# Reordered head loads and units, a later z row and fold, a fold over four PSUM banks, and a split last block in a four-layer transformer kernel

## Chip, cores and metric

The kernel runs on one core of one Trainium2 chip. The metric is the device time of one execution in microseconds (us). Executions of one kernel here differ by up to 0.2%, so each comparison below rests on several executions of both kernels on the same chip. All executions told of are fast: none is over 1.5% above the fastest of its kernel. Each execution also has a span, from its first to its last instruction, which lies 1.9 to 2.6 us under its time, and a clock, the mean share of its full speed that TensorE was granted.

## The reference, cut to what matters

`x` is 2048 tokens by 1024 channels in bf16. Two linear-attention blocks alternate with two gated feed-forward blocks, each behind a layernorm and with a residual.

```python
def _A_ref(x, wqkv, wo):                      # 32 heads of 32
    q, k, v = split_heads(x @ wqkv)
    phi = lambda t: jnp.where(t > 0, t + 1, jnp.exp(t)) + 1e-6
    pq, pk = phi(q), phi(k)
    kv = jnp.einsum("bhsd,bhse->bhde", pk, v)
    z = jnp.einsum("bhsd->bhd", pk)
    num = jnp.einsum("bhqd,bhde->bhqe", pq, kv)
    den = jnp.einsum("bhqd,bhd->bhq", pq, z)[..., None] + 1e-6
    return merge_heads(num / den) @ wo
def _B_ref(x, W_gate, W_up, W_down):
    return (relu(x @ W_gate) * (x @ W_up)) @ W_down
x = x + _A_ref(_layernorm(x), A_wqkv, A_wo);  x = x + _B_ref(_layernorm(x), ...)   # twice
```

## The kernel before

TensorE does all products; a unit is a 128 x 512 output, eight matmuls of 512 columns. `x` is cut into 16 blocks of 128 tokens. In the first layer the head loads weights and `x` in an order chosen by hand, normalizes the first four blocks on VectorE, transposes them on TensorE and starts the value units:

```python
        k0, k1, v0, v1 = (ring.place() for _ in range(4))
        self.load_x(0, 0)
        self.load_x(0, 1)
        v0(0, H)
        self.load_x(1)
        v0(H, 2 * H)
        v1()
        self.load_x(2)
        self.load_x(3)
        k0()
        self.load_x(4)
        # ... (cut) x 5 to 7, k1, x 8 to 15
        with tc.manual_schedule(engines={mybir.EngineType.DVE, mybir.EngineType.Activation}):
            for j in range(QT):                    # the first four blocks
                for c in range(2):
                    self.ln_stat(j, src[j], c, stats[j])
                r = self.ln_rstd(stats[j])
                # ... (cut) scale and transpose
```

A key unit is evicted in three steps, `exp` on ScalarE, then two on VectorE; the last one writes `pkv`, which the matmuls of `kv_step` read. GpSimd adds the keys up in `ksum`. A query unit takes three ScalarE steps and one on VectorE:

```python
            nc.scalar.activation(out=e, in_=ps, func=ACT.Relu, scale=-1.0)
            nc.scalar.activation(out=e, in_=e, func=ACT.Exp, scale=-1.0)
            nc.scalar.activation(out=e, in_=e, func=ACT.Identity, bias=self.eps6[:, 0:1])
            nc.vector.scalar_tensor_tensor(out=pq[:, c * NW:(c + 1) * NW], in0=ps, scalar=0.0,
                                           in1=e, op0=ALU.max, op1=ALU.add)
```

`z_row` casts `ksum` on ScalarE (`hi`) and spreads it with two matmuls of ones. `fold_wo` multiplies the transposed kv into the output weights: sixteen matmuls, two after each of eight query units, whose results are copied out of PSUM alternately by VectorE and ScalarE. `later.at(n, f)` runs `f` after n further units.

```python
        def fold_wo(i):
            n2, g = divmod(i, G)
            # ... (cut)
            ps = self.ps3.tile([P, NW], F32, tag="b")          # two banks
            nc.tensor.matmul(ps, lhsT=kvT[:, g, :], rhs=ring.get((l, f"o{n2}"))[:, g, :],
                             start=True, stop=True)
            dst = T[g // 2][:, g % 2, n2 * NW:(n2 + 1) * NW]
            if g % 2:
                nc.scalar.activation(out=dst, in_=ps, func=ACT.Copy)
            else:
                nc.vector.tensor_copy(out=dst, in_=ps)
        # ... (cut)
        with self.tc.manual_schedule(engines={mybir.EngineType.DVE,mybir.EngineType.Pool}):
            ring.free_before((l, "v0"))
            later.at(4, z_row)
            run(q_of(0, 4), v_then_kv(2))
            # ... (cut)
            def with_fold(u, i):
                return lambda: (u(), fold_wo(2 * i), fold_wo(2 * i + 1))

            run(q2[:5])
            run([with_fold(u, i) for i, u in enumerate(q2[5:] + q3[:5])])
            run(q3[5:], out0[:3])
            run(out0[3:])
```

Where `manual_schedule` names an engine, the instructions inside it keep the order of the program in that engine's queue (others can still be put between them); elsewhere the framework's scheduler orders it by a model of its own. Either way each engine's order is fixed before the kernel runs.

Of the kernel before, what the change touches and what calls it, by code (L numbers as in the profile page):

```python
# [7 lines left out]
ALU = mybir.AluOpType  # L8
ACT = mybir.ActivationFunctionType
F32 = mybir.dt.float32  # L10
BF16 = mybir.dt.bfloat16
PSUM = bass.MemoryType.PSUM
P = 128
# [65 lines left out]
class _Net:  # L79
# [85 lines left out]
    def head(self):  # L165

        nc, tc, ring = self.nc, self.tc, self.ring
        H = self.KT // 2

        zero = self.ep.tile([P, NW], BF16, tag="e")  # L170
        nc.vector.memset(zero, 0.0)
        idle = self.ps3.tile([P, NW], F32, tag="b")
        for _ in range(10):
            nc.tensor.matmul(idle, lhsT=zero[:, 0:P], rhs=zero, start=True, stop=True)
# [4 lines that stand above are left out]
        v0(0, H)  # L179
        self.load_x(1)  # L180
        v0(H, 2 * H)
        v1()
        self.load_x(2)
        self.load_x(3)
        k0()
        self.load_x(4)
        self.load_x(5)
        self.load_x(6)
        self.load_x(7)
        k1()  # L190
        for t in range(8, self.ST):
            self.load_x(t)
        ring.load_to(5)
        src = self.xb
        self.xnT[0, 0] = self.xnTp.tile([P, self.KT, QT * P], BF16, tag="xnT", name="xnT0_0")
        stats = [self.small.tile([P, 2, nc.vector.BN_STATS_DIM], F32, tag="stats", name=f"st{j}")
                 for j in range(QT)]

        def turn(j, xn, h):
            tp = self.ps3.tile([P, H, P], BF16, tag="b")  # L200
            for i in range(H):
                kt = h * H + i
                nc.tensor.transpose(tp[:, i, :], xn[:, kt * P:(kt + 1) * P], self.ident)
            dst = self.xnT[0, 0][:, h * H:(h + 1) * H, j * P:(j + 1) * P]
            if h == 0:
                nc.vector.tensor_copy(out=dst, in_=tp)
            else:
                nc.scalar.activation(out=dst, in_=tp, func=ACT.Copy)

        with tc.manual_schedule(engines={mybir.EngineType.DVE, mybir.EngineType.Activation}):  # L210
            for j in range(QT):
                for c in range(2):
                    self.ln_stat(j, src[j], c, stats[j])
                r = self.ln_rstd(stats[j])
                xn = self.xnp.tile([P, self.D], BF16, tag="xn")
                for h in range(2):
                    if j == 0 or h == 0:
                        self.ln_scale(src[j], *r, xn, h if j == 0 else None)
                    turn(j, xn, h)

    def ln_turn(self, layer, t, xn):
# [42 lines left out]
    def layer_A(self, l, last_ln):  # L264
# [107 lines left out]
        def fold_wo(i):  # L372
            n2, g = divmod(i, G)
            if n2 == 0 and g % 2 == 0:
                T.append(self.slab.tile([P, 2, D], BF16, tag="slab", name=f"T{l}_{g // 2}"))
            ps = self.ps3.tile([P, NW], F32, tag="b")
            nc.tensor.matmul(ps, lhsT=kvT[:, g, :], rhs=ring.get((l, f"o{n2}"))[:, g, :],
                             start=True, stop=True)
            dst = T[g // 2][:, g % 2, n2 * NW:(n2 + 1) * NW]
# [4 lines that stand above are left out]
# [19 lines left out]
        def q_of(sc, lag):  # L403
            return [lambda j=j, c=c: q_unit(sc, j, c, lag) for j in range(QT) for c in range(H)]
# [4 lines left out]
        def v_then_kv(q):  # L409
            u = column_major(v_unit, q)  # L410

            def last(j):
                u_j = u[QT + j]
                return lambda: (u_j(), later.at(2, lambda: kv_step(q * QT + j)))

            return u[:QT] + [last(j) for j in range(QT)]
# [10 lines left out]
        def run(*lists):  # L427

            n = max(len(u) for u in lists)
            for i in range(n):  # L430
                for u in lists:
                    if i < len(u):
                        u[i]()
                        later.tick()
# [7 lines left out]
        first = column_major(v_unit, 0)  # L442
        if l == 0:

            first = [first[c * QT + j + i] for i in (0, 2) for c in range(H) for j in range(2)]
        run(first)
        run(k_then_kv(0))
        run(column_major(v_unit, 1))
# [5 lines left out]
        run(k3[QT:])  # L454
        with self.tc.manual_schedule(engines={mybir.EngineType.DVE,mybir.EngineType.Pool}):
            ring.free_before((l, "v0"))
            later.at(4, z_row)
            run(q_of(0, 4), v_then_kv(2))
            run(q_of(1, 1), v_then_kv(3))
            ring.free_slowly((l, "q0"), later, 4)  # L460
            later.at(2, finish_kv)
            q2, q3, out0 = q_of(2, 1), q_of(3, 1), out_of(0)

            def with_fold(u, i):
                return lambda: (u(), fold_wo(2 * i), fold_wo(2 * i + 1))

            run(q2[:5])
            run([with_fold(u, i) for i, u in enumerate(q2[5:] + q3[:5])])
            run(q3[5:], out0[:3])
            run(out0[3:])  # L470
            ring.free_slowly((l, "o0"), later, 4)
            self.ln_later(last_ln, 0, 5, 4, 3)
            for sc in range(1, self.NQ):
                run(out_of(sc))
# [12 lines left out]
    def layer_B(self, l, final):  # L487
        nc, KT, D = self.nc, self.KT, self.D
        ring, later = self.ring, self.later
        for q in range(self.NQ):  # L490
            if q + 1 < self.NQ:
                self.ln_later(l, q + 1, 8, 8, 4)
            elif not final:
                self.ln_later(l + 1, 0, 8, 8, 4)
            hT = []
            for fc in range(self.F // NW):
                ring.free_before((l, q, "g", fc))
                wg, wu = ring.get((l, q, "g", fc)), ring.get((l, q, "u", fc))
                h = self.slab.tile([P, 4, NW], BF16, tag="slab", name=f"hT{l}_{q}_{fc}")
                hT.append(h)  # L500
                for fi in range(4):
                    pg = self.ps.tile([P, NW], F32, tag="a")
                    pu = self.ps3.tile([P, NW], F32, tag="b")
                    for w, ps in ((wg, pg), (wu, pu)):
                        for kt in range(KT):
                            nc.tensor.matmul(ps, lhsT=w[:, kt, fi * P:(fi + 1) * P],  # L506
                                             rhs=self.xnT[l, q][:, kt, :],
                                             start=(kt == 0), stop=(kt == KT - 1))
                        later.tick()
                    rg = self.ep.tile([P, NW], F32, tag="e")  # L510
                    nc.scalar.activation(out=rg, in_=pg, func=ACT.Relu)  # L511
                    nc.vector.tensor_tensor(out=h[:, fi, :], in0=pu, in1=rg, op=ALU.mult)  # L512
            for n2 in range(D // NW):
                acc = [self.ps.tile([P, NW], F32, tag="a", name=f"acc{l}_{q}_{n2}_{j}")
                       for j in range(QT)]
                for dg in range(4):
                    ring.free_before((l, q, "d", n2, dg))
                    wd = ring.get((l, q, "d", n2, dg))
                    for j in range(QT):
                        t = q * QT + j  # L520
                        for k in range(7):
                            ft = dg * 7 + k
                            nc.tensor.matmul(acc[j], lhsT=hT[ft // 4][:, ft % 4, j * P:(j + 1) * P],  # L523
                                             rhs=wd[:, k, :], start=(ft == 0),
                                             stop=(ft == self.FT - 1))
                        later.tick()
                        if dg < 3:
                            continue
                        xs = self.x[t][:, n2 * NW:(n2 + 1) * NW]
                        if not final:  # L530
                            nc.vector.tensor_tensor(out=xs, in0=xs, in1=acc[j], op=ALU.add)  # L531
                        else:
                            xo = self.ep.tile([P, NW], BF16, tag="e")
                            nc.vector.tensor_tensor(out=xo, in0=xs, in1=acc[j], op=ALU.add)  # L534
                            nc.scalar.dma_start(out=self.o_v[:, t, n2 * NW:(n2 + 1) * NW], in_=xo)

    def run(self):
        nc = self.nc
# [55 lines left out]
```

## Time and profile before

| | before |
|---|---|
| time at first, 3 executions | 1647.96 us median (1647.94 to 1648.34) |
| the execution that was profiled | 1649.5 us, span 1647.2 us |
| TensorE busy | 1634.7 us, 99% |
| lost stream time of TensorE, start to start | 13.7 us |
| from the last matmul's drawn end to the end | 3.3 us |

"Lost" is the time from one matmul's start to the next, less what a matmul of its width takes in steady flow in these traces (215.8 ns for 512 columns, 109 for 256, 55 to 56 for 128), summed. The prediction counts the `x` blocks from 0: its block 2 is the third.

### The profile page before, as it was taken

The numbers are of one execution on the slowest core, as the hardware profiler recorded it, in microseconds if no ns is written. First come the engines' busy times: TensorE is split into PE (matmuls) and PEld (weight loads), VectorE is DVE, ScalarE is ACT, GpSimd is POOL, SyncE is SP. The second block draws the span as 40 slices with busy tenths as digits, with TensorE's granted clock in tenths as the row PEclk, the third lists the DMA queues.
The fourth block names the chain that finished last, engine by engine and source line by source line (L and its number), as shares of the span: only waits on it lengthen the run. The fifth ranks groups of instructions, "written<-read, shape, count | busy, mean of one in ns | idle before, by whom it ended". The sixth has DMA issues, their size and how long they took to land.

```text
span 1647.2 us, 18687 instructions
## 1 busy us (share of the span) xinstructions
PE 1634.7 (99%) x7758; PEld 747.5 (45%) x7758; DVE 575.1 (35%) x930; ACT 372.2 (23%) x699; POOL 196.5 (12%) x102
## 2 busy tenths in 40 slices
PE   8999999999999999999999999999999999999999
PEld 4444444444444444444444444444444444444444
DVE  7664876223111321322146557852112112211111
ACT  4356702101110210111033675121011101101110
POOL 0355700000000000000013566000000000000000
PEclk9999999999999999999999999999999999999999
DMA  9113726446445644644530236274544464455442
GB/s 281 26 52 74 163 57 173 150 157 187 152 142 163 174 151 156 173 150 142 173 77 1 65 95 155 52 204 144 166 150 153 160 197 146 142 163 164 154 160 70
DMA packets 297907, 227.17 MB, mean 138 GB/s; under 512 B 103136, under 2 KB 295904, under 8 KB 297824
## 3 DMA queue, kind: packets, MB, share of 16 engines
q1 hardware_dynamic: 293216, 221.80, 46.3%
q10 hardware_dynamic: 4608, 4.20, 0.8%
q8 instruction: 60, 0.98, 0.2%
q14 instruction: 23, 0.19, 0.0%
HBM read 197.13 MB, written 4.19 MB: 122 GB/s over the span
## 4 chain that ended last, share of the span: by engine, by line
PE 91%; DVE 3%; ACT 2%; POOL 1%; issue 0%; DMA 0%; DVEq 0%; POOLq 0%
PE acc L523 23%; PE pu L506 23%; PE pg L506 23%; PE ps L284 13%; PE ps L389 7%; POOL ksum L299 1%; DVE e L244 1%; PE kv L311 1%; DVE pkv L245 1%; ACT e L347 0%; ACT e L346 0%; ACT T L381 0%; ACT e L348 0%; DVE pq L349 0%; DVE den L361 0%
## 5 line engine op out<-in xcount | busy, mean ns | idle before, releaser
L506 PEld LDWEIGHTS <-t 128*128 128x128 bf16 x3584 | 350.7, 98 | 422.8
L506 PE MATMUL pu<-xnT,t 128*128 128x512 bf16 x1792 | 423.3, 379 | 0.0
L506 PE MATMUL pg<-xnT,t 128*128 128x512 bf16 x1792 | 423.3, 379 | 0.0
L523 PE MATMUL acc<-t,hT 128*128 128x512 bf16 x1792 | 388.1, 379 | 0.0
L512 DVE TENSOR_TENSOR hT<-pu,rg 128x512 bf16<-128x512 f32 x224 | 154.6, 690 | 571.8 <-PE pu L506 571.8
L284 PE MATMUL ps<-t,xnT 128*128 128x512 bf16 x1536 | 344.7, 380 | 1.7 <-DMA t<-in_A_wqkv_dram 0.9
L511 ACT ACTIVATE rg<-pg 128x512 f32<-128x512 f32 x224 | 133.6, 596 | 737.5 <-PE pg L506 737.4
L523 PEld LDWEIGHTS <-hT 128*128 128x128 bf16 x1792 | 175.3, 98 | 211.5
L284 PEld LDWEIGHTS <-xnT 128*128 128x128 bf16 x1536 | 149.0, 98 | 177.7 <-issue 5.6
L389 PE MATMUL ps<-T,pqT 128*128 128x512 bf16 x512 | 111.5, 379 | 0.0
L143 ACT ACTIVATE rstd<-mv,eps 128x1 f32<-128x1 f32 x64 | 18.8, 294 | 335.4 <-DVE mv L141 335.4
L297 POOL CAST ksum<-pkv 128x1024 f32<-128x1024 bf16 x2 | 2.3, 1136 | 684.5 <-DVE pkv L245 684.5
L534 DVE TENSOR_TENSOR xo<-x,acc 128x512 bf16<-128x512 f32 x32 | 22.0, 687 | 171.1 <-PE acc L523 171.1
L136 DVE BATCH_NORM_STATS2 stats<-x 128x6 f32<-128x512 f32 (+1 forms) x120 | 78.3, 670 | 0.7
L389 PEld LDWEIGHTS <-pqT 128*128 128x128 bf16 x512 | 50.1, 98 | 60.4
L356 POOL TENSOR_TENSOR prod<-pq,zrow 128x1024 f32<-128x1024 bf16 x32 | 68.1, 2128 | 53.4 <-DVE den L361 35.5
L531 DVE TENSOR_TENSOR x<-x,acc 128x512 f32<-128x512 f32 x32 | 21.6, 676 | 149.5 <-PE acc L523 148.4
L299 POOL TENSOR_TENSOR ksum<-ksum,pkv 128x1024 f32<-128x1024 f32 x30 | 65.5, 2182 | 68.9 <-DVE pkv L245 67.7
L349 DVE SCALAR_TENSOR_TENSOR pq<-ps,e 128x512 bf16<-128x512 f32 x64 | 43.4, 679 | 82.0 <-ACT e L348 81.7
L244 DVE TENSOR_SCALAR e<-e 128x512 f32<-128x512 f32 x64 | 52.7, 823 | 48.9 <-ACT e L243 48.5
L367 POOL TENSOR_TENSOR pq<-pq,den 128x1024 bf16<-128x1024 bf16 x32 | 61.2, 1911 | 17.9 <-issue 10.6
L243 ACT ACTIVATE e<-ps 128x512 f32<-128x512 f32 x64 | 38.1, 596 | 70.9 <-PE ps L284 69.6
(44 smaller groups left out, 483.7 us busy)
## 6 DMA issues: line engine op xcount, KB each, us to landing
t<-in_B_W_gate_dram SPq DMA_DIRECT2D x56, 1024.0 KB, 6.9
t<-in_B_W_up_dram SPq DMA_DIRECT2D x56, 1024.0 KB, 5.4
t<-in_B_W_down_dram SPq DMA_DIRECT2D x64, 896.0 KB, 5.2
t<-in_A_wqkv_dram SPq DMA_DIRECT2D x11, 1024.0 KB, 5.2
t<-in_A_wo_dram SPq DMA_DIRECT2D x4, 1024.0 KB, 5.2
out_dram<-xo ACTq DMA_DIRECT2D x32, 128.0 KB, 2.2
x<-in_A_x_dram SPq DMA_DIRECT2D x15, 256.0 KB, 7.7
t<-in_A_wqkv_dram SPq DMA_DIRECT2D x2, 512.0 KB, 4.9
```

The lines of the kernel that those rows point to most:

```text
L136: self.nc.vector.bn_stats(out=stats[:, c, :], in_=src[:, c * fmax:(c + 1) * fmax])
L244: nc.vector.tensor_scalar(out=e, in0=e, scalar1=1.0, scalar2=1e-6, op0=ALU.min, op1=ALU.add)
L284: nc.tensor.matmul(ps, lhsT=self.xnT[l, l_q][:, kt, j * P:(j + 1) * P], rhs=w[:, kt, :], start=(kt == 0), stop=(kt == KT - 1))
L299: nc.gpsimd.tensor_tensor(out=ksum, in0=ksum, in1=pk[t], op=ALU.add)
L349: nc.vector.scalar_tensor_tensor(out=pq[:, c * NW:(c + 1) * NW], in0=ps, scalar=0.0, in1=e, op0=ALU.max, op1=ALU.add)
L356: nc.gpsimd.tensor_tensor(out=prod, in0=pq, in1=zrow, op=ALU.mult)
L367: nc.gpsimd.tensor_tensor(out=heads(pq), in0=heads(pq), in1=den[:, :].unsqueeze(2).to_broadcast([P, D // HD, HD]), op=ALU.mult)
L389: nc.tensor.matmul(ps, lhsT=pqT[sc][:, g, j * P:(j + 1) * P], rhs=T[g // 2][:, g % 2, n2 * NW:(n2 + 1) * NW], start=(g == 0), stop=(g == G ...
L506: nc.tensor.matmul(ps, lhsT=w[:, kt, fi * P:(fi + 1) * P], rhs=self.xnT[l, q][:, kt, :], start=(kt == 0), stop=(kt == KT - 1))
L511: nc.scalar.activation(out=rg, in_=pg, func=ACT.Relu)
L512: nc.vector.tensor_tensor(out=h[:, fi, :], in0=pu, in1=rg, op=ALU.mult)
L523: nc.tensor.matmul(acc[j], lhsT=hT[ft // 4][:, ft % 4, j * P:(j + 1) * P], rhs=wd[:, k, :], start=(ft == 0), stop=(ft == self.FT - 1))
```

## The change

It aims at the four places in which TensorE waits: the third x block, the cast of the key sum, the transposed kv with the two fold banks, and the tail. Cut to its core:

```diff
         v0(H, 2 * H)
+        self.load_x(2)
         v1()
-        self.load_x(2)
         self.load_x(3)
...
-                for h in range(2):
-                    if j == 0 or h == 0:
-                        self.ln_scale(src[j], *r, xn, h if j == 0 else None)
+                for h in (0, 1) if j == 0 else (None,):
+                    self.ln_scale(src[j], *r, xn, h)
+                for h in range(2):
                     turn(j, xn, h)
...
-            ps = self.ps3.tile([P, NW], F32, tag="b")
+            pool, tag = (self.kvp, f"kv{g // 2 % 2}") if g % 2 else (self.ps3, "b")
+            ps = pool.tile([P, NW], F32, tag=tag, name=f"fold{l}_{i}")
...
-            first = [first[c * QT + j + i] for i in (0, 2) for c in range(H) for j in range(2)]
+            first = [first[c * QT + j] for c, j in ((0, 0), (0, 1), (1, 0), (0, 2), (1, 1), (1, 2),
+                                                    (0, 3), (1, 3))]
...
-            later.at(4, z_row)
-            run(q_of(0, 4), v_then_kv(2))
+            later.at(5, z_row)
+            run(q_of(0, 5), v_then_kv(2))
...
-            run(q2[:5])
-            run([with_fold(u, i) for i, u in enumerate(q2[5:] + q3[:5])])
-            run(q3[5:], out0[:3])
-            run(out0[3:])
+            run(q2[:6])
+            run([with_fold(u, i) for i, u in enumerate(q2[6:] + q3[:6])])
+            run(q3[6:], out0[:2])
+            run(out0[2:])
...
+                if final and q == self.NQ - 1 and n2 == D // NW - 1:
+                    acc[QT - 1] = [self.kvp.tile([P, NW], F32, tag=f"kv{i}", name=f"acc_last{i}")
+                                   for i in range(2)]
```

The last block's two accumulators of 256 columns are finished one after the other, each with its own add and store (`add_down`).

More of the change, by code (lines that the diff above doesn't have):

```diff
@@ L513, in layer_B @@
             for n2 in range(D // NW):
-                acc = [self.ps.tile([P, NW], F32, tag="a", name=f"acc{l}_{q}_{n2}_{j}")
+                acc = [[self.ps.tile([P, NW], F32, tag="a", name=f"acc{l}_{q}_{n2}_{j}")]
                        for j in range(QT)]
+                if final and q == self.NQ - 1 and n2 == D // NW - 1:
+                    acc[QT - 1] = [self.kvp.tile([P, NW], F32, tag=f"kv{i}", name=f"acc_last{i}")
+                                   for i in range(2)]
                 for dg in range(4):
@@ L520, in layer_B, with add_down @@
                         t = q * QT + j
-                        for k in range(7):
-                            ft = dg * 7 + k
-                            nc.tensor.matmul(acc[j], lhsT=hT[ft // 4][:, ft % 4, j * P:(j + 1) * P],
-                                             rhs=wd[:, k, :], start=(ft == 0),
-                                             stop=(ft == self.FT - 1))
-                        later.tick()
-                        if dg < 3:
-                            continue
-                        xs = self.x[t][:, n2 * NW:(n2 + 1) * NW]
-                        if not final:
-                            nc.vector.tensor_tensor(out=xs, in0=xs, in1=acc[j], op=ALU.add)
-                        else:
-                            xo = self.ep.tile([P, NW], BF16, tag="e")
-                            nc.vector.tensor_tensor(out=xo, in0=xs, in1=acc[j], op=ALU.add)
-                            nc.scalar.dma_start(out=self.o_v[:, t, n2 * NW:(n2 + 1) * NW], in_=xo)
+                        parts = acc[j]
+                        n = NW // len(parts)
+                        for i, ps in enumerate(parts):
+                            for k in range(7):
+                                ft = dg * 7 + k
+                                nc.tensor.matmul(ps[:, 0:n],
+                                                 lhsT=hT[ft // 4][:, ft % 4, j * P:(j + 1) * P],
+                                                 rhs=wd[:, k, i * n:(i + 1) * n], start=(ft == 0),
+                                                 stop=(ft == self.FT - 1))
+                            if dg == 3:
+                                self.add_down(t, n2 * NW + i * n, ps[:, 0:n], final)
+                        later.tick()
+    def add_down(self, t, c, acc, final):
+        nc, n = self.nc, acc.shape[1]
+        xs = self.x[t][:, c:c + n]
+        if not final:
+            nc.vector.tensor_tensor(out=xs, in0=xs, in1=acc, op=ALU.add)
+            return
+        xo = self.ep.tile([P, NW], BF16, tag="e")
+        nc.vector.tensor_tensor(out=xo[:, 0:n], in0=xs, in1=acc, op=ALU.add)
+        nc.scalar.dma_start(out=self.o_v[:, t, c:c + n], in_=xo[:, 0:n])
     def run(self):
```

## The prediction

> **What bounds the kernel now.** I read the page first, for the engine that sets the end.
>
> ```profile
> span 1647.2 us, 18687 instructions
> PE 1634.7 (99%) x7758; PEld 747.5 (45%) x7758; DVE 575.1 (35%) x930; ACT 372.2 (23%) x699; POOL 196.5 (12%) x102
> PE 91%; DVE 3%; ACT 2%; POOL 1%; issue 0%; DMA 0%; DVEq 0%; POOLq 0%
> ```
>
> TensorE is the bound, and the change removes none of its work, so only its holes and slow stretches can be won. Busy time overstates: matmuls overlap, each is drawn 379 ns long but starts 216 ns after the one before (in the steady middle eight take 1.727 us, 0.2158 each). I therefore count lost stream time, start to start less 0.2158 for 512 columns and 0.055 for 128. That is the printed idle plus 0.16 us, as 379 - 216 ns of each printed idle is hidden behind the drawn end. Summed over the trace from the first matmul (2.1 us) it is 13.7 us: 7.5 before 20 us, 0.8 at 46, 0.9 at 107 and again at 922, 1.6 in 160 to 200 and 1.6 in 980 to 1004; the two feed-forward layers lose nothing. A tail of 3.4 us follows the last matmul. So 2% (33 us) isn't there to be won. Next, who TensorE waits for:
>
> ```profile
> PE idle L174 <- DVE zero L171: 2.1, 1, 2.1
> PE tp L203 <- DVE xn L152: 2.1, 1, 2.1
> PE ps L322 <- ACT hi L319: 1.5, 2, 0.7
> PE ps L284 <- DMA t<-in_A_wqkv_dram: 0.9, 1, 0.9
> PE ps L284 <- DVE xnT L206: 0.8, 2, 0.5
> PE ps L377 <- DMA kvT<-kvm: 0.6, 2, 0.3
> PE kv L311 <- DVE pkv L245: 0.6, 1, 0.6
> ```
>
> Lines 2, 3 and 6 are what the change aims at. In the timeline of TensorE the second line is followed by more:
>
> ```profile
> 11.73 1.24 PE L284 MATMUL ps<-t,xnT 128*128 128x512 bf16 x5
> 15.04 1.03 PE L203 MATMUL tp<-ident,xn 128*128 128x128 bf16 x8 [2.07 <-DVE xn L152]
> 15.87 4.66 PE L284 MATMUL ps<-t,xnT 128*128 128x512 bf16 x15
> 20.36 0.61 PE L203 MATMUL tp<-ident,xn 128*128 128x128 bf16 x8
> ```
>
> Fifteen matmuls take 20.36 - 15.87 = 4.49 us where 15 x 0.2158 = 3.24 would do, and the eight transposes 0.83 instead of 0.44: after the hole TensorE ran at half speed for a while. The table of stretches shows the clock (the 0.66 of the first row, third figure from its end) and two other engines that are full:
>
> ```profile
> 15.00:20.00 5.00, 4.96 (x22) 2.49 (x23) 3.58 (x9) 1.58 (x4) 0.00 (x0) 0.66 1.07 367
> 30.00:40.00 10.00, 10.00 (x54) 4.76 (x52) 9.97 (x23) 4.68 (x13) 0.68 (x1) 1.00 1.09 197
> 171.30:190.10 18.80, 18.19 (x82) 7.81 (x82) 16.26 (x28) 18.38 (x33) 16.16 (x9) 1.00 0.48 112
> ```
>
> VectorE (third pair) is busy 9.97 of 10 us in 30 to 40, ScalarE (fourth) 18.38 of 18.80 in the fold. These two limit what the change can give.
>
> [...] half clock from 15.0 to 18.4, with matmuls 427 ns apart[...]
>
> ```profile
> 41.02 4.89 POOL L299 TENSOR_TENSOR ksum<-ksum,pkv 128x1024 f32<-128x1024 f32 x2 [0.45 <-DVE pkv L245]
> ...
> 43.84 2.35 DVE L152 TENSOR_SCALAR xn<-x,mv,rstd 128x1024 bf16<-128x1024 bf16 x1
> ```
>
> This normalization takes 0.55 us elsewhere; here it ends at 46.19, just after the GpSimd sum. The last key eviction behind it holds TensorE at 46.06 (last line of the waits).
>
> **Part 1, the head.** Loads land in order at about 370 GB/s: second half of the v0 weights 8.61, v1 11.61, third x block 12.29, fourth 12.97. A block costs 12.97 - 12.29 = 0.68, so moved ahead of v1 it lands at 8.61 + 0.68 = 9.29 and v1 at 12.29. VectorE gets to it after its copy that ends at 10.37; before, statistics to normalized block took 12.31 to 14.99 = 2.68 us, so it is ready at 13.05 instead of 14.99. TensorE finishes v0 of blocks 0 and 1 at 10.42 + 8 x 0.216 = 12.15, and in the new order goes on with v1 of block 0 at 12.3 when v1 lands, until 14.0. The transposes of block 2 fit in there, and the hole and with it the half clock are gone. From 12.29: six units of 1.727 plus two sets of transposes at 0.45 end the eighth value unit at 23.55. Before: 64 - 34 matmuls are left at 20.81, so 20.81 + 30 x 0.2158 = 27.28. Gross gain 3.7. (The reordered scaling of block 0 moves its second half some 0.4 us earlier on TensorE, but the v0 landing at 8.61 rules there: 0.)
>
> Not all of it stays. VectorE is full until 46.8 with layernorm of later blocks and key evictions, and block 4 lands at 16.65 as before, so that work can begin only some 0.6 us earlier than its 17.22, plus 1.0 of gaps that close and part of the 2.4 us for block 3 that move forward. If VectorE gains only 1.5 to 3.0 where TensorE gains 3.7, the wait at 46 grows by 0.7 to 2.2. The priority of the earlier key evictions and the chance that the 1.8 us collision with GpSimd falls elsewhere speak for the low side: I take 0.9 off. Net 2.8.
>
> **Part 2, z row a unit later.** Each layer loses 0.74 + 0.16 = 0.90 before the two matmuls of ones. A unit is 1.73 us, more than that, so the wait vanishes in both layers; ScalarE sat idle 2.3 us before the key-sum cast, so little moves in its place. 2 x 0.88 = 1.75. The denominators start a unit later too; GpSimd has 4.0 us of work per 6.9 us there, and the first consumer of a query block is far away.
>
> **Part 3, fold a unit later, over four banks.** The timeline of the first layer has the ends of the stage:
>
> ```profile
> 171.70 0.60 PE L377 MATMUL ps<-t,kvT 128*128 128x512 bf16 x2 [0.35 <-DMA kvT<-kvm]
> 190.09 1.89 PE L389 MATMUL ps<-T,pqT 128*128 128x512 bf16 x8
> ```
>
> The transposed kv landed at 171.65, and TensorE was there at 171.19: 0.51 lost (0.44 in the other layer). A unit later it would come at 172.9: gone, 0.95. In the stage 64 projection and 16 fold matmuls take 18.39 us instead of 80 x 0.2158 = 17.26: 1.12 lost (1.18 in the other), all of it waits for the eviction of one of two banks. With four each bank has two units, 4.3 us, instead of 2.16. But ScalarE bounds the rate: a unit's three activations start 1.90 us apart and an eviction adds about 0.5 every unit, with the 2.3 us per unit seen, against 2.16 on TensorE. Its lag, about 0.9 at the new first fold, grows by some 0.15 a unit to 2.0; with its own work and VectorE's last step the projection bank is free 5.1 to 6.4 us after its matmuls, and TensorE wants it again after about 5.6. So I expect 0.2 per layer to come back as waits of the projection. 2.3 - 0.4 = 1.9.
>
> **Part 4, last block in two parts.** Rows at the end:
>
> ```profile
> 1643.88 0.69 DVE L534 TENSOR_TENSOR xo<-x,acc 128x512 bf16<-128x512 f32 x1 [0.82 <-PE acc L523]
> 1644.60 0.34 ACTq L535 DMA_DIRECT2D out_dram<-xo  x1
> ```
>
> The store lands at 1646.32, 1.72 after its issue. Half the columns: a 1024-wide reduction takes 1.21 us and a 512-wide mask 0.68, so 1.03 ns an element, and 256 fewer save 0.26. [...] Net 0.25.
>
> **Sum.** 2.8 (head) + 1.75 (z row) + 0.95 (transposed kv) + 1.9 (banks) + 0.25 (end) = 7.65. 1647.96 - 7.65 = 1640.3; I say 1640.4.
>
> **Rivals.** (a) VectorE takes the head back: it stays the bound to 46 us and the kv wait grows from 0.73 to about 2.9; the 9.97 of 10 speaks for it[...]. Head net 1.5, time 1641.7. (b) ScalarE takes the fold back: 18.38 of 18.80 for it, the unused half of four projection banks against. Fold banks 0.5 instead of 1.9, time 1641.8. (c) The static order on TensorE puts block 2's transposes before v1 of block 0, and a hole of about 0.9 remains at 12.15, with half clock after it: 2 us less, 1642.4. (d) VectorE keeps up and the collision goes: head 4.4, time 1638.8. (a), (b) and (c) together: 1645.
>
> **Range.** The floor is all losses named gone with none coming back: 4.4 + 1.8 + 0.95 + 2.3 + 0.4 = 9.9, 1638.1. Upwards two rivals at once give 1643. Range 1638.0 to 1643.8. Faster by over 2% would need 33 us, twice all losses: 0.003. Slower by 33 us would need a new stall in the feed-forward layers, which aren't touched: 0.003.
>
> **What would show it.** After: no half clock between 5 and 40 us and no wait for the normalized block over 1 us (part 1); the eighth value unit done near 23.6; a kv wait near 46 - 3 us of about 1.6; no wait for the cast of the key sum (part 2); none for the transposed kv, and under 0.3 us per layer of bank waits in the fold (part 3); a last add of about 0.43 us (part 4). Wrong if the half clock stays, if a wait for projection banks after the fold passes 1 us, or if anything appears in the feed-forward layers.

## The result and the profile after

| | before | after |
|---|---|---|
| time, 6 executions each | 1648.26 us (1647.94 to 1648.52) | 1645.02 us (1644.53 to 1645.89) |
| ratio | | 0.9981, 95% interval 0.9968 to 0.9994 |
| span of the profiled execution | 1647.2 us | 1642.6 us |
| lost stream time | 13.7 us | 9.5 us |
| last matmul's drawn end to the end | 3.3 us | 3.0 us |

A ratio is the mean time of one kernel's fast executions over that of the other's in the same rounds, so not quite the ratio of the medians. The change gains 3.2 us, 0.2%. "Within 2%" was right, but 1645.0 lies above the stated range of 1638.0 to 1643.8: 7.6 us were predicted. The two spans and the two lost times are not a fair pair, since the profiled execution of before had a spell of half clock (granted clock 0.50 from 15.0 to 18.4 us, with 512-column matmuls 427 ns apart); in e0_before, the same kernel without it, they are 1645.3 and 11.9 us. The page of the changed kernel:

```profile
span 1642.6 us, 18754 instructions
PE 1632.7 (99%) x7786; PEld 749.8 (46%) x7786; DVE 575.8 (35%) x931; ACT 371.7 (23%) x699; POOL 196.3 (12%) x102
PE 94%; ACT 2%; DVE 1%; issue 1%; ACTq 0%
```

There are 28 matmuls more (the last block's halves) and TensorE still is the chain. Who it waits for, in the same view as before (us in total, times, longest):

```profile
...
PE tp L203 <- DVE xn L152: 1.5, 1, 1.5
PE fold L378 <- DVE T L384: 1.5, 4, 0.4
PE kv L311 <- DVE pkv L245: 0.6, 1, 0.6
```

The waits for the cast of the key sum and for the transposed kv are gone from this list. But the wait for a normalized block is still there with 1.5 us, the one for the key eviction with the same 0.6, and the fold waits for VectorE's copies. The timeline of TensorE in the head:

```profile
13.07 0.62 PE L203 MATMUL tp<-ident,xn 128*128 128x128 bf16 x8
13.53 3.40 PE L284 MATMUL ps<-t,xnT 128*128 128x512 bf16 x15
18.46 0.62 PE L203 MATMUL tp<-ident,xn 128*128 128x128 bf16 x8 [1.53 <-DVE xn L152]
```

The third block is transposed at 13.07 (predicted 13.1), at full clock. The hole has moved to the fourth block, whose transposes lose 1.69 us: the matmuls before them were through at 16.77. VectorE's timeline says why:

```profile
13.85 1.28 DVE L136 BATCH_NORM_STATS2 st<-x 128x6 f32<-128x512 bf16 x2
16.45 0.69 DVE L136 BATCH_NORM_STATS2 stats<-x 128x6 f32<-128x512 bf16 x1 [1.33 <-DMA x<-in_A_x_dram]
17.07 0.19 DVE L141 BATCH_NORM_AGGREGATE mv<-st 128x2 f32<-128x12 f32 x1
...
17.85 0.55 DVE L152 TENSOR_SCALAR xn<-x,mv,rstd 128x1024 bf16<-128x1024 bf16 x1
```

`st` belongs to the fourth block, `stats` to the fifth. The scheduler put the fifth block's first statistics, which lie outside the hand-ordered part, between the fourth block's statistics and its aggregate. The fifth block lands at 16.43. The fourth block's statistics are done at 15.13, yet its aggregate starts only at 17.07, behind the instruction that waited for the fifth block.

The fold, on TensorE:

```profile
170.38 0.59 PE L378 MATMUL fold<-t,kvT 128*128 128x512 bf16 x2
...
175.30 0.59 PE L378 MATMUL fold<-t,kvT 128*128 128x512 bf16 x2 [0.44 <-DVE T L384]
...
180.28 0.38 PE L378 MATMUL fold<-t,kvT 128*128 128x512 bf16 x1 [0.29 <-DVE T L384]
```

and on VectorE:

```profile
172.20 1.21 DVE L361 TENSOR_REDUCE den<-prod 128x32 f32<-128x1024 f32 x1
...
174.03 0.63 DVE L349 SCALAR_TENSOR_TENSOR pq<-ps,e 128x512 bf16<-128x512 f32 x1
174.57 0.68 DVE L384 CAST T<-fold 128x512 bf16<-128x512 f32 x1
```

The first even fold result is there at 170.8, yet it is copied out at 174.57, behind a reduction and the eviction of the query unit that stands before it in the program. That eviction itself waits for three ScalarE steps. The bank is wanted again two units later, at about 174.7, and the copy ends at 175.25.

### The profile page after: what moved, and what is told of

Its sections match the earlier page's. It is cut to its first block, busy times and chain, and to the rows that moved or that the text cites. A ratio compares the mean times of both kernels' runs of the same rounds, so it can differ in the third digit from the quotient of the medians.

```text
span 1642.6 us, 18754 instructions
## 1 busy us (share of the span) xinstructions
PE 1632.7 (99%) x7786; PEld 749.8 (46%) x7786; DVE 575.8 (35%) x931; ACT 371.7 (23%) x699; POOL 196.3 (12%) x102
## 4 chain that ended last, share of the span: by engine, by line
PE 94%; ACT 2%; DVE 1%; issue 1%; ACTq 0%
PE pg L508 24%; PE pu L508 24%; PE acc L532 23%; PE ps L284 16%; PE ps L390 7%; PE kv L311 1%; ACT e L347 1%; ACT e L346 1%; PE acc_last L532 0%; DVE den L361 0%; DVE pq L349 0%; ACT e L348 0%; PE fold L378 0%; DVE T L384 0%; DVE xn L152 0%
## 5 line engine op out<-in xcount | busy, mean ns | idle before, releaser
L532 PE MATMUL acc<-t,hT 128*128 128x512 bf16 x1764 | 382.5, 379 | 0.0
L284 PE MATMUL ps<-t,xnT 128*128 128x512 bf16 x1536 | 341.0, 379 | 1.0 <-DVE xnT L206 0.6
```

Of the source, the lines that this page charges most:

```text
L284: nc.tensor.matmul(ps, lhsT=self.xnT[l, l_q][:, kt, j * P:(j + 1) * P], rhs=w[:, kt, :], start=(kt == 0), stop=(kt == KT - 1))
L532: nc.tensor.matmul(ps[:, 0:n], lhsT=hT[ft // 4][:, ft % 4, j * P:(j + 1) * P], rhs=wd[:, k, i * n:(i + 1) * n], start=(ft == 0), stop=(ft ...
```

## The experiments

All gave correct results. Each has five timed executions beside nine of the kernel before on the same chip, in three groups: e0_before, p1_head, p3_foldlater and p4_banks (before: 1648.13 us median), p2_zrow, i1_x4, i2_split and i3_both (1648.23), and the other four (1647.96). "Lost" numbers come from start-to-start sums over each run's trace.

| run | time, us | ratio to before (95%) | lost to 20 us | key waits, 20 to 95 us | z row, both layers | kv and fold, both layers |
|---|---|---|---|---|---|---|
| e0_before | 1648.09 | 0.9998 (0.9985 to 1.001) | 5.5 | 0.9 | 1.8 | 3.3 |
| p1_head | 1647.71 | 0.9993 (0.998 to 1.0007) | 6.2 | 0.9 | 1.8 | 3.3 |
| p2_zrow | 1646.39 | 0.9987 (0.9974 to 1.0001) | 6.0 | 0.7 | 0.5 | 3.3 |
| p3_foldlater | 1649.04 | 1.0005 (0.9992 to 1.0017) | 6.1 | 0.7 | 1.8 | 4.2 |
| p4_banks | 1647.15 | 0.9992 (0.998 to 1.0005) | 5.8 | 0.7 | 1.8 | 2.6 |
| p6_last | 1647.87 | 1.0 (0.9988 to 1.0013) | 6.7 | 0.8 | 1.8 | 3.3 |
| the change | 1645.02 | 0.9981 (0.9968 to 0.9994) | 5.6 | 0.8 | 0.5 | 2.2 |
| i1_x4 | 1644.63 | 0.9976 (0.9964 to 0.9989) | 4.2 | 3.1 | 0.5 | 2.2 |
| i2_split | 1643.26 | 0.9968 (0.9955 to 0.998) | 6.3 | 0.8 | 0.5 | 0.5 |
| i3_both | 1643.02 | 0.9967 (0.9954 to 0.9979) | 4.4 | 1.4 | 0.5 | 0.5 |
| i5_act | 1642.90 | 0.9969 (0.9955 to 0.9982) | 4.5 | 1.9 | 0.5 | 0.5 |
| i6_manual | 1643.08 | 0.9969 (0.9957 to 0.9982) | 4.7 | 1.9 | 0.5 | 0.5 |
| i8_manual_z | 1643.13 | 0.997 (0.9958 to 0.9983) | 4.7 | 1.9 | 0.5 | 0.5 |

The change has the six executions of its own measurement.

**e0_before**: the kernel before again, no edit.

> The kernel before, unchanged, to see how often its head falls to half clock. Theory A ([...] the first profile caught it): most executions have a granted clock of 1.000 and a span of about 1645.6 us, 1.5 us under the profiled 1647.2, and only some have 0.999. Rival B (every execution has it, and the change's 4.6 us of span shrink to 3.2 of time for another reason): all executions show clock 0.999 and a span near 1647.2.

None of its five executions shows a clock under 1.000, and their spans run from 1645.3 to 1647.3 us. Among the other 27 executions of before three show 0.999; they took 1649.51, 1649.68 and 1650.29 us, the slow end. The first profile, with its 3.4 us at 0.50, has a mean of 0.999 too. If 0.999 stands for that spell, the half clock came in 3 executions of 32, and the first profile had caught one. (Counting all kernels with the old head, 5 of 52 executions show 0.999, and none of 41 with the new head. By chance alone none of 41 would come up about once in twenty, so it isn't shown that the change rids the head of it; at 1.5 us in one execution of ten it would be worth about 0.15 us on average.) Of rival B nothing is left, though spans of up to 1647.3 occur at full clock as well. In the trace of e0_before the head loses 5.5 us, where the first profile had 7.5:

```profile
14.39 0.62 PE L203 MATMUL tp<-ident,xn 128*128 128x128 bf16 x8 [0.70 <-DVE xn L152]
14.85 3.40 PE L284 MATMUL ps<-t,xnT 128*128 128x512 bf16 x15
```

The hole before the third block is 0.70 here instead of 2.07, and the 15 matmuls behind it run at full speed (3.40 us as drawn, for 4.66 in the first profile). In p2_zrow it cost 2.0 us and in p6_last 1.9, both at a clock of 1.000. So the size of the hole varies from execution to execution, and half clock followed the one of the first profile (2.2 us lost) but not these two; what decides between them was not shown.

**p1_head**: the head's three edits alone.

```diff
+        self.load_x(2)
         v1()
-        self.load_x(2)
# ... with the unit order and the scaling order of the change
```

> Only the head of the change (third x block ahead of the second value weights, the unit order, the scaling order). Theory A: as most executions of before have no half clock, the head gives only about 0.4 us: lost time before 20 us falls from about 5.9 to 5.6, with a new wait of some 1.5 us for the normalized fourth x block near 17 us, because VectorE's queue has statistics of the fifth block, still in flight, ahead of that block's aggregate. Rival B: 1.9 us less, as the two profiles differ there. The wait for the key eviction near 44 us stays at 0.7 in both.

It gains 0.42 us in the medians (1648.13 to 1647.71), and the interval includes nothing at all. Theory A's time held in the medians. Rival B's 1.9 finds no support there, nor in the traces below, but the interval alone, down to 0.998, would let it pass. The lost time did not fall to 5.6 but is 6.2, with 2.0 of it in the new wait for the fourth block and more before the second half of the v0 weights, which landed at 8.98 here.

Why does the earlier third block bring so little? VectorE. In both kernels the first statistics of the fifth block start when that block lands or soon after, at 16.36 in e0_before (landed 16.00) and at 16.45 after (16.43), and from there VectorE has no slack up to 45. Table of stretches, e0_before and then the changed kernel (the third pair is VectorE):

```profile
17.00:30.00 13.00, 12.90 (x66) 5.95 (x65) 12.88 (x32) 7.20 (x23) 0.00 (x0) 1.00 1.20 335
30.00:45.00 15.00, 14.27 (x87) 7.21 (x85) 14.94 (x30) 6.00 (x15) 6.05 (x3) 1.00 0.83 150
```

```profile
17.00:30.00 13.00, 11.54 (x60) 5.54 (x61) 12.88 (x32) 6.98 (x23) 0.00 (x0) 1.00 1.15 342
30.00:45.00 15.00, 14.40 (x89) 7.25 (x88) 15.00 (x30) 6.10 (x16) 6.05 (x3) 1.00 0.85 150
```

12.88 of 13 and 14.94 or 15.00 of 15 us. Then the fourth kv step of the first group waits for the last key eviction. In e0_before:

```profile
45.02 0.40 PE L311 MATMUL kv<-pkv 128*128 128x128 bf16 x4 [0.74 <-DVE pkv L245]
```

and after the change:

```profile
44.98 0.40 PE L311 MATMUL kv<-pkv 128*128 128x128 bf16 x4 [0.60 <-DVE pkv L245]
```

TensorE passes this point at 45.02 before and at 44.98 after. Over the traces without half clock it passes between 45.02 and 46.10 with the old head (five traces, mean 45.4) and between 44.98 and 45.75 with the new one (three, mean 45.5). In all eight, that is 28.5 to 28.7 us after the first statistics of the fifth block, wherever these start between 16.36 and 17.59. Whatever TensorE does sooner in the head, it waits here for the same VectorE work. And before 20 us the old head loses 6.0 us in the mean of its five traces, the new one 6.0 in the mean of its three.

Part of that VectorE work is a collision: the normalization just before the last key eviction takes 2.35 us in all eight instead of 0.55, beside GpSimd's key sum. (Of the fifteen normalizations of this form in the changed kernel's trace, the twelve that overlap no GpSimd instruction take 0.53 to 0.55 us; the three that do take 0.54, 0.66 and 2.35.) These 1.8 us are more than TensorE's wait of 0.7 to 0.9, so the wait would perhaps not be there without them; no run takes the collision away alone.

**p2_zrow**: the z row alone.

```diff
-            later.at(4, z_row)
-            run(q_of(0, 4), v_then_kv(2))
+            later.at(5, z_row)
+            run(q_of(0, 5), v_then_kv(2))
```

> Only the z row a unit later. Theory A (the wait moves from the key sum on GpSimd to ScalarE's queue, where the cast now stands behind one more query unit and value copy): lost time before the matmuls of ones falls from 0.90 to about 0.24 us a layer, 1.3 us less in all. Rival B (part of it is given back later by the denominators that start a unit later): 0.5 us less or nothing.

Lost time before the ones falls from 0.90 to 0.24 us a layer, as theory A had it, 1.3 us in both. The medians differ by 1.8; the rest is within the noise, and the interval just reaches 1. No sign shows that anything is given back. The 0.24 has a new cause, as ScalarE's timeline of the changed kernel shows:

```profile
109.55 0.58 ACT L304 ACTIVATE pkv<-ps 128x512 bf16<-128x512 f32 x1
110.03 1.05 ACT L319 ACTIVATE hi<-ksum 128x1024 bf16<-128x1024 f32 x1
```

GpSimd's key sum ends at 105.47 in that trace, so the cast could run 4.5 us earlier. It stands behind one more query unit and a value copy in ScalarE's queue.

**p3_foldlater** and **p4_banks**: the fold's two edits, each alone.

```diff
-            run(q2[:5])
-            run([with_fold(u, i) for i, u in enumerate(q2[5:] + q3[:5])])
-            run(q3[5:], out0[:3])
-            run(out0[3:])
+            run(q2[:6])
+            run([with_fold(u, i) for i, u in enumerate(q2[6:] + q3[:6])])
+            run(q3[6:], out0[:2])
+            run(out0[2:])
```

> Only the fold a unit later, with two banks as before. The wait for the transposed kv (0.51 and 0.44 us of lost stream) goes in both layers. Theory A (bank waits come from VectorE's fixed order, each copy behind the eviction of the unit before it, whose input comes from ScalarE): the bank waits stay at about 1.1 us a layer or grow by 0.2, so about 0.8 us less than before. Rival B (ScalarE's rate is the limit, and the stage ends when ScalarE ends): the later start lets ScalarE run ahead, so no part of the 0.95 comes through, 0 to 0.3 less.

```diff
-            ps = self.ps3.tile([P, NW], F32, tag="b")
+            pool, tag = (self.kvp, f"kv{g // 2 % 2}") if g % 2 else (self.ps3, "b")
+            ps = pool.tile([P, NW], F32, tag=tag, name=f"fold{l}_{i}")
```

> Only the four banks, at the old place of the fold. Theory A (VectorE's order): the even copies still come three to four us after their matmuls, so bank waits fall little, from 1.1 to about 0.9 us a layer; time within 0.5 us of before. Rival B (number of banks was the limit, as predicted): waits under 0.3 us a layer, 1.6 to 2.2 us less.

The later fold alone is no gain: 0.9 us slower in the medians, which the interval can't tell from nothing. Its trace shows the mechanism that both expectations missed. The wait for the transposed kv goes (0.44 us a layer), but the bank waits rise from 1.2 to 2.0 us a layer, most of it in front of the first copy on VectorE, which in that trace stands behind a query block's reduction and a further eviction; TensorE loses 1.00 us before 176.45. The four banks alone take the bank waits from 1.2 to 0.8 us a layer, near theory A's 0.9 and far from the 0.3 of rival B; the medians differ by 1.0 us, which the interval can't tell from nothing. Together, in the change, both leave 1.1 us a layer of 1.6: they gain 1.1 in the two layers together, where 2.85 was predicted.

**p6_last**: the last block in two parts, alone (the diff is the last part of the change and `add_down`).

> Only the last output block in two parts. The tail from the last matmul to the end falls from 3.3 to 2.95 us as in the changed kernel's profile, the last add from 0.69 to about 0.43; 0.07 us is lost in the narrower matmuls; 0.3 us less in all, at the edge of what the rounds can show. A rival (the two stores on one queue delay each other) would show a tail of 3.3 or more.

The tail is 3.0 us and the last add 0.42, as expected; the 14 matmuls of 256 columns start 109 ns apart. In the changed kernel's trace the mean is 109.2, so two of them take 2.6 ns more than one of 512 columns (215.8), 0.07 us for the 28 pairs. The medians differ by 0.09 us, which says nothing for or against a gain of 0.3. The tail can be read from fourteen profiles: 3.0 us in all eight with the two parts, 3.3 in all six without. Last add of the changed kernel:

```profile
1639.68 0.42 DVE L547 TENSOR_TENSOR xo<-x,acc_last 128x256 bf16<-128x256 f32 x1 [0.34 <-PE acc_last L532]
```

**i1_x4**: the changed kernel, with the fifth block ahead of the first key weights.

```diff
         self.load_x(3)
-        k0()
         self.load_x(4)
+        k0()
```

> The changed kernel with the fifth x block loaded ahead of the first key weights, so that it lands near 13.7 us instead of 16.4. Theory A (VectorE's queue is blocked by statistics of the fifth block, whose load has not landed, ahead of the fourth block's aggregate): the idle of 1.53 us before the fourth block's transposes falls to 0.4 or less, and the span by about 1.2 us. Rival B (VectorE is simply short of time until 45 us): TensorE comes earlier to the key evictions, their wait grows from 0.76 to about 2 us, and the time stays within 0.3 us of the changed kernel.

The hole before the fourth block's transposes closes (1.7 us lost become 0.26), as theory A said of its cause. But rival B told what follows: TensorE, now early, waits 0.5, 1.6 and 1.0 us for key evictions between 34 and 46. Part of these waits may have another cause: VectorE itself stood idle here for 1.39 us before 33.66, where the trace names the transfer that reads the normalized blocks, `xnT<-xn`. In i3_both, which has the same head, that idle is 0.09 and the waits are 0.4 and 1.0. The time is 0.4 us under the change's, from another group, so no clear gain. Both statements hold: the order of the queue made the hole, and VectorE's key evictions are the next thing that TensorE waits for.

**i2_split**: the changed kernel, with a query unit's fold matmuls and their copies between its projection and its activations.

```diff
             ps = project(f"q{c}", sc, j)
+            if between:
+                between()
...
-                return lambda: (u(), fold_wo(2 * i), fold_wo(2 * i + 1))
+                return lambda: u(lambda: (fold_wo(2 * i), fold_wo(2 * i + 1)))
```

> The changed kernel with the two fold matmuls and their copies put into a query unit between its projection and its activations: the same matmul order on TensorE, but each fold copy stands in VectorE's queue ahead of that unit's eviction instead of behind it. Theory A (VectorE's order makes the bank waits): lost time in the fold falls from 1.1 us a layer to 0.2 or less, 1.8 us less in all. Rival B (ScalarE's rate, 98% busy in the stage): the waits come back in the projection banks, and the time stays within 0.4 us of the changed kernel.

1643.26 us, 1.8 under the changed kernel (measured in another group), with 0.25 us a layer lost in the fold instead of 1.1. Nothing came back in the projection banks, so ScalarE's rate wasn't the limit, though it is busy 17.70 of 18.0 us there. The order of TensorE's matmuls and the banks are the same; what differs is the place of the copies, 32 places in VectorE's queue and 14 in ScalarE's. All four bank waits of the changed kernel's trace end 0.05 us after a copy on VectorE (in the first layer at 175.25 and 180.23), so VectorE's queue is the one that counts:

```profile
174.76 0.63 DVE L386 CAST T<-fold 128x512 bf16<-128x512 f32 x1
175.31 0.68 DVE L351 SCALAR_TENSOR_TENSOR pq<-ps,e 128x512 bf16<-128x512 f32 x1
```

The copy comes before the eviction now. It ends at 175.39, and the bank, filled by the matmul that starts at 171.11, is wanted again at 175.4. The copy's new place was tried with four banks alone; whether two would do then was not run.

**i3_both**: both edits.

> Both of these edits together. Theory A for both: 3.0 us less than the changed kernel, about 1642.0, faster than both kernels. If one of the rivals holds: 1.2 or 1.8 less. If both hold: the time of the changed kernel.

1643.02 us, 5.2 under the kernel before in its group. It is 0.2 under i2_split, so the fifth block's earlier load adds next to nothing, as rival B of i1_x4 has it. It beats the kernel before beyond its interval (0.9954 to 0.9979), and by 2.0 us in the medians the changed kernel, though those two did not run side by side.

**i5_act**: i3_both, with the key evictions of every second block of the first group done in three ScalarE steps.

```diff
+        if on_act:
+            nc.scalar.activation(out=e, in_=ps, func=ACT.Relu, scale=-1.0)
+            nc.scalar.activation(out=e, in_=e, func=ACT.Exp, scale=-1.0)
+            nc.scalar.activation(out=e, in_=e, func=ACT.Identity, bias=self.eps6[:, 0:1])
+        else:
+            nc.scalar.activation(out=e, in_=ps, func=ACT.Exp)
+            nc.vector.tensor_scalar(out=e, in0=e, scalar1=1.0, scalar2=1e-6, ...)
...
+                     l == 0 and q == 0 and j % 2 == 1)
```

> The third improved kernel (both edits), with the key evictions of every second block of the first group done in ScalarE's three-step form, so that VectorE has 4 x 0.41 us less to do before the key evictions that TensorE waits for. Theory C (in the head VectorE is short of time, and what TensorE gains it waits for at the key evictions, 0.4 us at 36 and 1.0 at 43): these waits fall by 1.0 us or more in sum and the span with them. Rival D (the waits come from single collisions of a normalization with GpSimd, not from a shortage): the wait near 43 stays at 1.0 and the time within 0.3 us of the third improved kernel.

The key waits did not fall: they were 1.9 us in sum against 1.4, and the time is within 0.1 us. The large one moved with the collision. In i3_both, 1.0 us is lost before 44.44, at the fourth kv step, after a normalization that takes 2.35 us from 41.44. Here the long normalization starts at 39.69, 1.0 us is lost before 42.70, at the third step, and 0.1 before the fourth. So theory C, that VectorE's sum of work is the limit, fails this test, and rival D fits: the wait follows the single collision. That the three ScalarE steps delay those evictions themselves may hide some of the relief; that wasn't told apart.

**i6_manual**: i3_both, with VectorE's order fixed by the program in the key and value stage.

```diff
-            self.ln_at((4 if l == 0 else 2) + 3 * (i - QT), l, i, 2)
+            self.ln_at((3, 5, 7, 12, 17, 18, 20, 21, 23, 27, 31, 35)[i - QT] if l == 0 else
+                       2 + 3 * (i - QT), l, i, 2)
...
+        with (self.tc.manual_schedule(engines={mybir.EngineType.DVE}) if l == 0 else ExitStack()):
+            run(first)
+            # ... the runs up to the last key units, indented
```

> The third improved kernel with VectorE's order in the first layer's key and value stage fixed by the program, the layernorms of later blocks put where value units run and not ahead of the key evictions; same work. Theory C' (VectorE has the time, but the scheduler's order puts layernorms of far blocks in front of key evictions): both key waits go, 1.2 to 1.4 us less than the third improved kernel, about 1641.7, and no wait for a transposed block appears. Rival C (VectorE's total work until 45 us is the limit): the waits stay or turn into a wait for a transposed block near 40 us; time within 0.4 us.

The waits before 50 us shrink to 0.3, as theory C' had it, but 1.2 and 0.4 us appear at 73 and 93, and the time is the same. The wait at 73 has two rows behind it, GpSimd's and VectorE's:

```profile
66.16 6.65 POOL L299 TENSOR_TENSOR ksum<-ksum,pkv 128x1024 f32<-128x1024 f32 x3 [21.21 <-DVE pkv L245]
```

```profile
71.38 1.71 DVE L152 TENSOR_SCALAR xn<-x,mv,rstd 128x1024 bf16<-128x1024 bf16 x1 [0.60 <-ACT rstd L144]
```

A normalization of 0.55 us takes 1.71 while GpSimd adds keys until 72.81. Layernorms that are moved out of the head land beside the key sums of the second group. Its five executions differ by 0.08 us only (1643.02 to 1643.10), against 1.6 in i3_both; one reading, which I have not tested, is that a later wait takes up the head's differences.

**i8_manual_z**: i6_manual with `later.at(6, z_row)` and `q_of(0, 6)`.

> The kernel with VectorE's order fixed, and the z row one more unit later. If what is left of the z row's wait (0.24 us a layer) is only ScalarE's queue, it goes: 0.4 to 0.5 us less. If the denominators, again a unit later, delay anything, no gain.

No gain, and not a test either: the queue orders of TensorE and ScalarE around the z row, which the scheduler makes, came out the same as in i6_manual, with the cast at 110.27 and 0.24 us lost. What a cast further up in the queue would give stays open.

## Why the prediction was wrong, point by point

- **The baseline.** The step "Fifteen matmuls take 20.36 - 15.87 = 4.49 us ... after the hole TensorE ran at half speed" read a true row, but of a rare execution. It took 1649.5 us against a median of 1648.0, and I took its losses off that median. About 1.6 us of the predicted gross gain existed in about 1 execution in 10.
- **Part 1, the step that failed:** "the statistics to normalized block took ... so it is ready at 13.05" was right (13.01). The sum that follows, which ends the eighth value unit at 23.55, took it that the fourth block would be ready in time. It was not, by 1.69 us, and the unit ends at 25.4 (25.3 in e0_before). "Not all of it stays ... I take 0.9 off. Net 2.8" was wrong: TensorE passes the last key wait at 44.98 instead of 45.02, so net 2.8 became 0 in the traces, and 0.4 in p1_head's medians. What the runs show in its place: VectorE begins the later blocks when the fifth one lands, 16.4 before and after, and TensorE gets the last keys 28.5 to 28.7 us later with either head.
- **Part 1, its rivals:** I had found this bound and put it down as rival (a), with a net of 1.5 and a wait that grows to 2.9; the wait stayed at 0.8, since TensorE had lost its lead at the fourth block already. My "1.5 to 3.0" for VectorE was true of the first profile, in which TensorE passes at 46.85, 1.87 later than after; but in that profile VectorE began at 17.22 and had 1.0 us of gaps, and e0_before has neither. Nor did "the chance that the 1.8 us collision with GpSimd falls elsewhere" come true: in the changed kernel as before, the normalization just before the last key eviction takes 2.35 us (41.98 to 44.33).
- **Part 2:** right in mechanism. Its size was 1.33 (2 x 0.67) for 1.75, since a query unit and a value copy more of ScalarE's queue stand before the cast. The step that failed is "ScalarE sat idle 2.3 us before the key-sum cast, so little moves in its place".
- **Part 3:** the transposed kv is gone as predicted, 0.9 to 0.95 us. "With four each bank has two units, 4.3 us, instead of 2.16" was true of the banks, but the copies come 4.2 us after their matmuls, so 1.1 us a layer stays where 0.2 was expected. I had taken the lag from ScalarE alone, and not read the order of VectorE's queue, which the program fixes. i2_split shows it: with the copies earlier in the queue, 0.85 us a layer went. Of the 1.9 for the banks about 0.2 came in the two layers together (2.4 us of bank waits became 2.2). Rival (b), 0.5, came nearer, with the wrong engine.
- **Part 4:** right in the trace; p6_last's times are too coarse to show it. The last add is 0.42 (0.43 predicted), the tail 0.3 less (3.3, where the prediction put 3.4, became 3.0; 0.05 of it is the store), and the narrower matmuls are 109 ns apart where 512 columns take 215.8, so they cost 0.07 us more in all.
- **The sum, term by term:** head 0 to 0.4 for 2.8, z row 1.33 for 1.75, fold and kv 1.1 for 2.85, end 0.3 for 0.25: 2.7 to 3.1 for 7.65, and 3.2 measured. The spans agree: e0_before's profile at 1645.3 and the change's at 1642.6 are 2.7 apart. That rivals (a), (b) and (c) together gave 1645 in the prediction is luck: the hole of (c) did not stay where (c) had it, the wait of (a) did not grow, and of the banks less came than (b) said.

What stays open: why the second half of the v0 weights lands between 7.9 and 9.2 us in different executions, which moves the head by up to 1 us, and how far the key waits can be packed away; three different orders of VectorE's work gave the same time within 0.2 us.

## What to carry to other kernels

Before taking a loss from one profile, compare that execution's own time with the median. Follow a saved wait to the next point where engines meet, and ask what releases TensorE there: if that engine starts and ends its work at the same moments, the saving stops there, as at 44.98 us here (45.02 before). Read where the copy that frees a buffer stands in its engine's queue before adding buffers: here two banks more took the bank waits from 1.2 to 0.8 us a layer, and moving the copy ahead of the eviction that waits, with four banks, took the loss from 1.1 to 0.25.
